# Two short groups of matmuls on a constant tile in the opening of a two-layer transformer kernel, and a new order of all its operations

## The chip, the cores and the metric

The kernel runs on one core of one Trainium2 chip. The core has a matrix engine (TensorE, in the profile PE, its weight loads PEld), a vector engine (VectorE, DVE), a scalar engine (ScalarE, ACT), GpSimd (POOL), and a queue on SyncE (SP) that starts the DMAs. Each engine works through its own list of instructions in order and waits on semaphores for the others. The metric is the time of one execution on the device in microseconds, less being better.

## What is computed

Two kinds of blocks are applied in turn, twice: sliding-window attention with 32 heads of 16 dimensions and a window of 256, and a token-mixing MLP across the 2048 positions.

```python
S, D, F, H, W = 2048, 512, 1792, 32, 256
def A(x):                                   # attention
    q, k, v = split(x @ wqkv)               # 32 heads of 16
    s = q @ k.T * 16 ** -0.5, kept where 0 <= i - j < W
    return softmax(s) @ v @ wo
def B(x):                                   # MLP over positions
    h = layernorm(x)
    u = gelu(einsum("sd,sf->df", h, w1) + b1)
    return (einsum("df,fs->ds", u, w2) + b2).T
for _ in range(2):
    x = x + A(layernorm(x))
    x = x + B(layernorm(x))
```

All inputs are bf16; x is 2048 by 512.

## The kernel before

x stays in SBUF as 16 blocks of 128 positions (`x_sb`). The program first builds a list of 2476 operations (`Graph.op`, line 107): an operation is one or several instructions of one engine, with the tiles that it reads and writes. The order in which they are put on the engines is not found when the kernel is built: the string `ORDER` (lines 15 to 42) holds a permutation of the list, and for each operation the choice among its alternative engines (`alts`: for example a copy on DVE or ACT, a mask on POOL or DVE). `begin_order` (line 44) unpacks it, `replay` (line 175) puts the operations on their engines in this order and gives out the buffers, and `emit` (line 196) works out the semaphore waits. So every engine's list, the DMA queue's included, follows from that string.

The stages. Attention goes by chunks of 64-position blocks (`CHUNKS`, line 331). For a chunk, `ln_blocks` (line 478) normalises blocks of x: `bn_stats` and `bn_aggr` on DVE, the power -1/2 on POOL (line 484), the subtraction and product on DVE (line 491) into `xh_sb`. `qkv` (line 535) transposes them into `xhT`, for the first 512 positions on PE (`f_tr`, line 547, four transposes of 128x128 into one PSUM bank, copied out at line 556 or 558 by DVE or ACT), later by DMA (line 542). Then `proj` multiplies by column blocks `o` = 0 to 3 of the weights of K and Q (line 513 is the matmul helper for all of these), and `vproj` by those of V. In the first layer the first 512 positions are handled in two halves of 256 (`split`, line 643).

`attention` (line 664) issues score groups (line 690), exponentials on ACT (line 705), masks on POOL or DVE (line 726), probability times value (line 747), a transposition and division by the sum (lines 767 to 778). There are 152 score groups in all. V reaches its layout `vb` by a store of four DMAs (line 636, operation `vz`). `wo_block` multiplies by `wo` and adds to x. Parts of the MLP's first product (`u_part`, line 842) and its second product (`y_block`, line 901) serve as other work for PE between score groups. `u_last` (line 861) is the rest of the first product with the gelu.

The opening. SP's first DMAs are `load_x` (line 400) and `load_w` (line 404). Weights are loaded in column parts: K and Q each as columns 0 to 255 (`o` = 0, 1) and 256 to 511 (`o` = 2, 3), V whole. SP's order in the string of before is: x block 1, x block 0, x blocks 2 and 3, K columns 0 to 255, Q columns 0 to 255, x blocks 4 to 7, Q columns 256 to 511, K columns 256 to 511, V, the two biases, x blocks 8 to 11, and so on. PE begins with `f_warm` (line 390), 36 matmuls of 128x128 on a tile of ones, a part of `uT` that the MLP overwrites much later. After them come, in the order of before: transposes of block 1, transposes of block 0, K o=0, Q o=0, Q o=1, K o=1, the first score group, transposes of block 3, transposes of block 2, Q o=3, the second score group, Q o=2, K o=2, the third score group, K o=3.

Of the kernel before, what the change touches and what calls it, by code (L numbers as in the profile page):

```python
# [11 lines left out]
P = 128  # L12


ORDER = (
    'c-qBQJ&5a87Cw^iym#m24ro9DE$D$>P@zHr1r$&~4;*kn0Tl{p!G#}q!G!|~IH1A-2lN&PwBQ9TIN-tyE*x;-!V50EV3sLdcwrV?xbVUhQ@EI7Sf+5{!o?nq'
    '$20ciz5Hx8yJyB%_g-CH-SeIAd`ALMAW$=FmRTW@UM>_MC=^Pi;EO_mPE}Ps8;@00Q*G-bFh2xcf8YPD^Jy4{4r?wJVNeNZF(i;5j)u<AALc&kTb8BtuoYXD'
    'EV9&YSZ!4!>!g`bN{ewkFV?-!CZqniE{d#Ft%9xV!b#)(TCEaPYV5=_a)q2Md&JD;Y}-<ZEX(4%qNtz|nGh-nqM(nNFd2`>41lrbFj=oV>y08w5=@sO5l;Q9'
    'E5~t`4k7c4g`?**4MwApcs`k)PYEH@>2%p2_m%ug%J;zU^<}w}Bmj_HTwbUu%%gUDrPRKHF)ZpZ8V-j>IkgT#q9zGxwOWL+*Q6H5QAD5FVugcBIS8UCVtAx5'
    'oJ<&u19$iv7cna1#_*YKJ5^OyJ|z~OtkC_q)3F@aao}aY-|XcJja+V-4ePd#=6Nr5$8=54^GwtKgfnf&d1+c%n=zA#x^CzI129br?M|l+Elo!hRD}YZf_Qqu'  # L20
    'SP)3ERD?p|W-T+p<AlWmmz&J>+$%~ixu#_`=S`xiFBAY-2B_6)1cnJql2x_3URO7ptD9B5K6*wd)Vkd{-aVgQFQ<Q>cFUdVVsW`#OsA3K%;)o&*{hi55Q9-J'
    '&$FfBG&||^{?_aDDLp%bAP7veKNy<kcP63}C9PHz{n0aH$ElgsxDhjE)LBq-b-g0Gt{ca(`sEk$b^TQ&DrE65;-xkz7100?E&w~1%|a*V<m_xVrnDCQ9!bX-'
    'm1YXX*h}M)fU!Om&@okIOl(PvC5<{j12J|S3bq}Tigu~!`;_{gMNNZdeg7q;j;bwzsGwS!B?u~0Ziq%Y!^?{V8oI8Zce{fD0`^>Em^H0dLzbj46plFn<Ww=A'
    'FQK`4LOj>DNP1RH&t|jQXq06s1sG+39kbi*t^uyE!Cc~!i-kgzrhK_Xo{tGG>%nMzHqPfML1rY`Bx!fr#C02P^EJAFZ(cjutY58xXXjs)hPF-A3lBL3pX4lJ'
    'o4RQ@9~cBgQ$#}$1OcwgE@B2$AdHBjArra3DN3SFkg5WD1k-axgz>l%2E(u)1b&%$CBINMT;FsZMb~r1oPiq~IYiJfbj!AeLw#WAgbe9`w0dBuuGqvgRI6$j'
    'Lc4<2z`#YeO+!o3Fn0_>IzT9qQcL7U7do+6@7L?yx^*Vrn%pXe80Su@MFqwhm|>=H;=0V37#a(!ArlQI2rlNJAe`WqOfhG#%;{=H-5W~sx^x5=7q*a+gflh$'
    'eZw$Pt#TZr6a%Qw`y4VQmouyne9JOS0EC7qvVzDPj44PKNl{G8B<pp1eIlAyme0J)%S%H$)eL|an)+N(`aLv4B*F~_HO#v|s2W6@$RDsi$nbjkB_tw<aCUYk'
    '2%!wcfUen!F_|78BN06ngymAB$TM;-Nt5|()|t)vvzaWn&qvv;Tm`7MhvtWaKA@`N30<K-=(ly9A_Jd|R8$)In<f)_y+1(=bS0n$TwlMwx<cq7j=u@(C`omM'
    's+WpyhcVx0`At5b6!LM*{CvrmDw0$xmkNc#rysW*%d#2dEs#FcKqmsA;wpwx&^1K`SfV3>fB;P<6ID1nqf~>FlQsVIBw?qUO$1{_QR7&{n2;j^pNrDz@KvRP'
    'TuK<mIr4oZ1y_!9SyUwYJ76btI<*!T3yU5b?QZw{9Hy=d9K2`0HxPs}^t#>t;Lp8&uVtQFrU}$Q`lqt{ZNl~Yf`ICa&~-Y75XsujO{=A87$B%rB7GV}b(9zY'  # L30
    '!{`(WoNg6MMP0AzkT0PA69N(@pXYm16Wzfq^z*(fYqEw}a{7X?cLkw<Ig%y~Rv3X&ok}t$2N6%!f^;N~$NkaC$qf0x1Uyf>-6bt(Dr%$g90?}?KF5_9Bjq&r'
    '9VRfOm7H#+>+RW`V$C>FkB<j`i7}q|K(_<XYPW`Ah;7)b*Etl+sQ&d=xDeCKb@TZ=swXnG*RcqAC>3m#2FEZ|10}nJyGwXDa!fJMLOcUE@4D;t8rCTF_KdDp'
    '|1^yA<<&pVaphmfWICUu<!>~UB*XY_G#-s?$tqjlN}AScVXSKL*K!D9S_VJ=yjH4~LRu`AgEE#cl(BpvpVe)WwLK4sNQCSM`bXp=iwJ^1G+BAkm!89|;E<#0'
    '5m!-^W`k?os-6+90>f~bsiaDi{tQqkm1!RJ6VNdN6KJ;<Xrpm^*cw#FsDIU@*6DORRU@vZyI^4JQ7JM?MU+}7R=i5t^UGK(hjfISwCi<9P;1@T^KGmPwx6?$'
    '*`}Si72oo#we1*=ty>Z<K|oE*NRs|kQo3VFj-qBWDr2RP%}Py=YhYMbK*X6DDpU<N!bV@P(lwST5xh&(i+Q7GS|c{pKw4GeK!HfSMw)Ln+D&j%-rOMigkF)W'
    'tIbAOU&8!+J`XM&6!y_r8jXS!q*_hOK?T1v(t@EBna)rd<f<%4h$aS4NQ;jOl%l*~OW_w9_o&0&&v3hj+gnZ!duhI<*Czn)Jlx^9hb0`)bV%+FN`XV$Zku+n'
    '%>ZN|?LN&sO}kq=zHOhv-X((zp6<=U-J8*Pa_H5QU5DrIHq7vcHy#^*d!K)d4tMK5e>l${9Ua~EIN<K_y7Py7!t>njX^wjX)W6uc-L~877SOvn4xM=XCjR#3'
    'ffxM4i0An?kYc;%9Wwk|$-{APJ07>ksr#_L-FWzK8n-+D0aDygj{&!b@9tr^=Pk!^+<%y7KZ6b2k1gcj|6*(}X#Cwjf54*cklzn(I)3MF&FvFM_fPP5OiFd)'
    'PDWB$dFT6#-?q>0yM*KRNS1zT!}g1NyGbT<D<hdyr!twhb1?I;1+K~*&h7>o9{)0XkL(?vf4BgDKjPoOZ+@F@{L_OaPq}pBkzPEK;jMa+EjG7q-XVq8Cxq-~'
    'fqY-CA5M)9kj(yDwjO2Pn4mw1SmuWW<UnaM{7ypdNwS?t+e|9Z`@ub6^$)5i|0od;xd4x4`DbU#p|J1k!A{$`U5U8saSyKSuRIv-&+SBsdzd5tlMLqG#I842'  # L40
    'njg9Q>mP6%x*dvl<9p-|jZg3K-1a{$!)bv|s~^WdEIxed;iHG!)%)G|$*<zszX32A5e)'
)

def begin_order(n):
# [208 lines left out]
def mm_cost(n, cols):  # L253
    return n * (cols / 2.4 + 4.0)
# [50 lines left out]
def bass_interleave_layers__sliding_block__mixer_token_mlp__prompt_kernel(  # L305
# [11 lines left out]
    S, D = A_x.shape[1], A_x.shape[2]  # L317
    F = B_w1.shape[1]
# [16 lines left out]
    with es:  # L335
# [9 lines left out]
        vb = sb("vb", [P, 3, 8, 16, 17])  # L345
# [6 lines left out]
        uT = sb("uT", [P, NFT, 512])  # L352
        w1b = sb("w1b", [P, 4, NT // 2, 256])
        w2b = sb("w2b", [P, 2, 4096])
        ident = sb("ident", [P, P])
# [14 lines left out]
        op = g.op  # L370
# [16 lines left out]

        warm = Tile(banks)

        def f_warm(e):  # L390
            for _ in range(36):
                last = e.matmul(PS[:, warm.slot, 0:P], lhsT=uT[:, 0, 0:P], rhs=uT[:, 0, 0:P], start=True, stop=True)
            return last
        op("vector:wm", lambda e: e.memset(uT[:, 0, 0:P], 1.0), writes=["uT0"], cost=100)
        op("tensor", f_warm, reads=["uT0"], writes=[warm], cost=2000, prio=-1, cfg="f", cls="f")

        x_src = A_x.rearrange("b (t p) d -> p (b t) d", p=P)
# [100 lines left out]
        def bank(t, i=0):  # L498
            return PS[:, t.slots[i], :]
# [7 lines left out]
        def fprio():  # L507
            return 1e6 + len(g.ops)
# [10 lines left out]
        def mm_group(kind, dst, n, mk, reads, cols=512, step=2, prio=None, holds=(), after=()):  # L519

            prio = fprio() if prio is None else prio
            for k0 in range(0, n, step):
                k1 = min(n, k0 + step)

                def f(e, cols32, k0=k0, k1=k1):
                    last = None
                    for k in range(k0, k1):
                        last = matmul(e, cols32, *mk(k), start=(k == 0), stop=(k == n - 1))
                    return last
                rd = reads(k0, k1) if callable(reads) else reads  # L530
                op("tensor:" + kind, f, reads=rd, writes=[dst], cost=mm_cost(k1 - k0, cols), prio=prio, holds=holds, after=after, cfg="f",
                   cls="f", flex=True)


        def qkv(m, before, split, layer):
# [3 lines left out]
            def transpose(i, wide):  # L539
                t = 4 * m + i  # L540
                if wide is None:
                    op("sync:tr", lambda e: e.dma_start_transpose(xhT[:, tx.slot, :, i * P:(i + 1) * P], xh_sb[:, t, :]),
                       reads=[f"xh{t}"], writes=[(tx, i)], dma=True, cost=1700, issue=1600.0, prio=-1e5)
                    return
                ft = filler(True)

                def f_tr(e):
                    for c in range(4):
                        last = e.transpose(bank(ft).bitcast(dt.bfloat16)[:, c * P:(c + 1) * P],
                                           xh_sb[:, t, c * P:(c + 1) * P], ident[:])  # L550
                    return last
                op("tensor:ftr", f_tr, reads=[f"xh{t}", "ident"], writes=[ft], cost=4 * 60, prio=fprio(),
                   holds=[tx], cfg="f", cls="f")
                src = lambda: bank(ft).bitcast(dt.bfloat16)[:, 0:512].rearrange("p (c n) -> p c n", c=4)
                dst = lambda: xhT[:, tx.slot, :, i * P:(i + 1) * P]
                op("vector:evt", lambda e: e.tensor_copy(dst(), src()), reads=[ft], writes=[(tx, i)],
                   cost=dve_cost(512, 0.5, psum=True), prio=-2e5,
                   alts=[("scalar", lambda e: e.copy(dst(), src()), act_cost(512))])

            def proj(o, which, a, b, wide):  # L560

                n, key = b - a, (filler(m == 0), which)
                ft = key[0]
                at = lambda: bank(ft)[:, 0:n]
                staged = m > 0 or (not layer and (o, a) in STAGED)
                ts = Tile(p_stg) if which and staged else None
                mm_group("fk" if which else "fq", key, 4, lambda c: (
# [75 lines left out]
            for a, b in ((0, 256), (256, 512)) if split else ((0, 512),):  # L643
                first = m == 0 and a == 0
                late_stats[:] = [first_k[0]] if m == 0 and not layer and not first else []
                before([4 * m + i for i in range(a // P, b // P)], first)
                late_stats[:] = []
                for i in range(a // P, b // P):
                    transpose(i, first if m == 0 and not layer else None)
                for which in (1, 0):  # L650
                    proj(0, which, a, b, first)
                vs = list(range(a // P, b // P))
                vproj(vs[0])
                for o in range(1, 4):
                    for which in (1, 0):
                        proj(o, which, a, b, False)
                if vs[2:]:
                    vproj(vs[2])
# [330 lines left out]
```

## Time and profile before

| | us |
|---|---|
| median of the runs of before | 437.09 |
| the runs | 437.09, 436.16, 437.51 |
| the profiled execution, its own time | 436.27 |
| span of that execution, first to last instruction | 434.5 |
| PE busy in the span | 420.9 |
| DVE busy | 322.6 |
| ACT busy | 317.0 |
| POOL busy | 187.2 |

The page of the profile gives busy times over the span, the granted TensorE clock in 40 slices (all of them at full speed here), the chain of work that ended last and the costliest groups of instructions. The timeline lists instructions in order of time, neighbours of one line merged, with the idle time of the engine before them and what ended it. The windows give each engine's busy time in a stretch. A matmul's record includes the time that its results need to drain, so PE shows as busy across small gaps; the starts of successive matmuls show the pace.

### The profile page before, as it was taken

To read this page: it belongs to the slowest core of one execution; us is meant where nothing else is said; L and a number is where in the kernel's file an instruction comes from. 1 tells how busy PE (TensorE), PEld (TensorE's weight loads), DVE (VectorE), ACT (ScalarE), POOL (GpSimd) and SP (SyncE) were. 2 spreads that over 40 slices of the span, in tenths; PEclk is the share of its full clock that TensorE was granted. 3 is DMA by queue.
4 is the path that set the end of the run, shared out by engine and by line. 5 is a ranking of instruction groups with operands and counts; after the bars stand their busy time and mean duration, and the time that the engine had idled before them with its cause. 6 is when DMAs were issued, how large, how long until landed. Compare 5 with 4: busy or idle time off the path is not lost.

```text
span 434.5 us, 14318 instructions
## 1 busy us (share of the span) xinstructions
PE 420.9 (97%) x6177; PEld 188.5 (43%) x6177; DVE 322.6 (74%) x629; ACT 317.0 (73%) x364; POOL 187.2 (43%) x277
## 2 busy tenths in 40 slices
PE   7979989999999999999999999999999999999997
PEld 6534333434444444444444444444434444445443
DVE  7998989779996678556777999989788758422205
ACT  5999999999997953606999999899999870520000
POOL 7788865864664620011465554365435221000000
PEclk9999999999999999999999999999999999999999
DMA  8565262302163257723542282240223262747713
GB/s 237 167 125 88 63 127 37 79 5 49 26 166 83 75 152 211 208 62 88 137 110 52 64 147 64 51 77 11 47 64 99 66 175 69 226 140 213 228 32 115
DMA packets 101850, 46.03 MB, mean 106 GB/s; under 512 B 32156, under 2 KB 101788, under 8 KB 101788
## 3 DMA queue, kind: packets, MB, share of 16 engines
q1 hardware_dynamic: 101788, 45.13, 41.7%
q8 instruction: 49, 0.80, 0.8%
q14 instruction: 13, 0.11, 0.1%
HBM read 33.56 MB, written 2.10 MB: 82 GB/s over the span
## 4 chain that ended last, share of the span: by engine, by line
PE 73%; ACT 18%; DVE 6%; DMA 1%; POOL 1%; issue 0%; SPq 0%
PE PS L513 50%; ACT pt L705 17%; PE PS L868 8%; PE PS L690 8%; PE PS L747 7%; DVE stats L471 1%; DMA vb<-vst 1%; DVE xh_sb L491 1%; DVE pt L726 1%; DVE rl L767 1%; DMA x_sb<-in_A_x_dram 1%; POOL pt L726 0%; DVE stg L594 0%; DVE vst L631 0%; SPq L636 0%
## 5 line engine op out<-in xcount | busy, mean ns | idle before, releaser
L705 ACT ACTIVATE pt<-PS 128x1024 bf16<-128x1024 f32 (+1 forms) x304 | 281.0, 1036 | 13.1 <-PE PS L690 11.9
L726 POOL TENSOR_TENSOR pt<-pt,ldm 128x256 int32<-128x256 int32 (+2 forms) x189 | 125.9, 686 | 101.7 <-ACT pt L705 101.1
L513 PE MATMUL PS<-xhT,wqkv 128*128 128x512 bf16 (+1 forms) x288 | 67.8, 357 | 2.7 <-ACT pt L705 1.9
L513 PE MATMUL PS<-xh_sb,w1b 128*128 128x512 bf16 x280 | 69.9, 381 | 0.1
L513 PE MATMUL PS<-uT,w2b 128*128 128x512 bf16 (+2 forms) x308 | 68.3, 360 | 0.0
L690 PE MATMUL PS<-qT,kbd 32*128 32x64 bf16 (+4 forms) x1552 | 60.2, 247 | 3.1 <-ACT pt L705 2.1
L484 POOL TENSOR_TENSOR rstd<-agg,mhalf 128x2 f32<-128x2 f32 (+1 forms) x33 | 23.8, 722 | 66.8 <-DVE agg L473 66.7
L909 DVE SCALAR_TENSOR_TENSOR x_sb<-PS,bcol,x_sb 128x512 bf16<-128x512 f32 x31 | 22.6, 746 | 38.0 <-PE PS L513 37.7
L690 PEld LDWEIGHTS PS<-qT,kbd 32*128 32x128 bf16 x1552 | 22.7, 92 | 61.7 <-ACT pt L705 45.6
L767 DVE STREAM_TRANSPOSE rl<-PS 128x1024 f32<-128x1024 f32 x32 | 39.9, 1248 | 12.3 <-PE PS L747 12.1
L747 PE MATMUL PS<-pt,vb 64*17 64x128 bf16 (+4 forms) x3104 | 43.6, 248 | 2.4 <-DMA vb<-vst 1.1
L471 DVE BATCH_NORM_STATS2 stats<-x_sb 128x6 f32<-128x512 bf16 x64 | 44.2, 693 | 1.5 <-DMA x_sb<-in_A_x_dram 0.8
L883 ACT ACTIVATE uT<-rl,bcol 128x512 bf16<-128x512 f32 x28 | 18.3, 712 | 33.8 <-DVE rl L879 33.8
L513 PEld LDWEIGHTS PS<-uT,w2b 128*128 128x128 bf16 x308 | 27.5, 98 | 31.1 <-issue 3.2
L747 PEld LDWEIGHTS PS<-pt,vb 64*17 64x17 bf16 x3104 | 31.8, 84 | 17.6 <-issue 7.9
L513 PE MATMUL PS<-uT,pt 128*128 128x512 bf16 x168 | 39.2, 379 | 0.0
L868 PE MATMUL PS<-xh_sb,w1b 128*128 128x512 bf16 x168 | 37.7, 379 | 0.0
L513 PEld LDWEIGHTS PS<-xhT,wqkv 128*128 128x128 bf16 x288 | 24.2, 97 | 30.1 <-issue 6.3
L513 PEld LDWEIGHTS PS<-xh_sb,w1b 128*128 128x128 bf16 x280 | 23.7, 98 | 30.8 <-issue 5.9
L513 PE MATMUL PS<-wqkv,xhT 128*128 128x512 bf16 x128 | 34.2, 381 | 0.2 <-DVE stg L594 0.2
L726 DVE TENSOR_TENSOR pt<-pt,ldn 128x256 int32<-128x256 int32 (+1 forms) x77 | 29.6, 404 | 5.3 <-ACT pt L705 5.0
L513 PE MATMUL PS<-wo_sb,oT 128*128 128x512 bf16 x128 | 32.4, 380 | 0.5 <-ACT pt L705 0.5
(62 smaller groups left out, 340.7 us busy)
## 6 DMA issues: line engine op xcount, KB each, us to landing
w1b<-in_B_w_dram SPq DMA_DIRECT2D x112, 128.0 KB, 2.8
w2b<-in_B_w_dram SPq DMA_DIRECT2D x70, 128.0 KB, 2.8
pt<-in_B_w_dram SPq DMA_DIRECT2D x42, 128.0 KB, 3.0
vb<-vst SPq DMA_DIRECT2D x64, 68.0 KB, 2.1
out_dram<-x_sb SPq DMA_DIRECT2D x15, 128.0 KB, 1.8
x_sb<-in_A_x_dram SPq DMA_DIRECT2D x3, 512.0 KB, 6.2
kbd<-stg SPq DMA_DIRECT2D x80, 16.0 KB, 1.9
wqkv<-in_A_wqkv_dram SPq DMA_DIRECT2D x4, 256.0 KB, 5.4
```

The lines of the kernel that those rows point to most:

```text
L471: op("vector:stat", lambda e: e.bn_stats(st[:, 0:6], x_sb[:, t, :]), reads=[f"x{t}"], writes=[("st", i)], cost=dve_cost(512))
L484: op("gpsimd:rstd", lambda e: e.tensor_tensor(rstd[:, t0:t1, 0], agg[:, t0:t1, 1], mhalf[:, 0:1].to_broadcast([P, t1 - t0]), op=ALU.pow), ...
L491: op("vector:xh", lambda e: e.tensor_scalar(xh_sb[:, t, :], x_sb[:, t, :], agg[:, t, 0:1], rstd[:, t, :], op0=ALU.subtract, op1=ALU.mult), ...
L513: return e.matmul(o, lhsT=w, rhs=x, start=start, stop=stop, skip_group_check=True)
L690: last = e.matmul(bank(tt[r // 2], r % 2)[:, base + c0 * 64:base + (c0 + n) * 64], lhsT=kbd[32 * r:32 * r + 32, tk.slot, o, jj].rearrange( ...
L705: op("scalar:exp", lambda e, ts=ts, tp=tp, i=i, cols=cols: e.activation(probs(tp)[:, i, 0:cols, :], pair(ts)[:, :, 0:cols].rearrange("p r ...
L726: return e.tensor_tensor(v, v, m, op=by)
L747: last = e.matmul(bank(t, h)[32 * r:32 * r + 17, i + q0 * 64:i + (q0 + n) * 64], lhsT=vb[64 * h:64 * h + 64, tk.slot, jj, 4 * o + r, :], r ...
L767: op("vector:od", lambda e, t=tod, tr=tr: e.transpose(rl[:, tr.slot:tr.slot + 2].rearrange("p a b -> p (a b)"), pair(t)), reads=[(tod, i) ...
L868: last = e.matmul(bank(tu, tt), lhsT=v()[:, sc - b0, k0 + tt * P:k0 + (tt + 1) * P], rhs=xh_sb[:, sc, :], start=(sc == b0), stop=(sc == NT ...
L883: op("scalar:gelu", lambda e, ft=ft, tt=tt: e.activation(uT[:, ft, :], rl[:, tmps[tt].slot], ACTF.Gelu_apprx_tanh, bias=b1col[:, ft:ft + 1 ...
L909: op("vector:resy", lambda e: e.scalar_tensor_tensor(x_sb[:, t, :], bank(ft), b2col[:, t:t + 1], x_sb[:, t, :], op0=ALU.add, op1=ALU.add), ...
```

## The change

Three things change in the code, and the order string.

- `f_warm` takes a count and a bank, and `warm_more` issues it as an operation of its own: two matmuls of 128x128 before the second of the first two transposes, into the bank that this transpose then overwrites, and six before the first projection (K o=0), into that projection's bank. The two are tied by `after` to the transpose before them, and by their bank to the work behind them.
- The first two blocks are transposed in the order block 1, block 0 in the program's list (`[::-1]`).
- The order string is another one. It holds two operations more.

```diff
-        def f_warm(e):
-            for _ in range(36):
-                last = e.matmul(PS[:, warm.slot, 0:P], lhsT=uT[:, 0, 0:P], rhs=uT[:, 0, 0:P], start=True, stop=True)
+        def f_warm(e, n=36, t=warm):
+            for _ in range(n):
+                last = e.matmul(PS[:, t.slot, 0:P], lhsT=uT[:, 0, 0:P], rhs=uT[:, 0, 0:P], start=True, stop=True)
             return last
         op("vector:wm", lambda e: e.memset(uT[:, 0, 0:P], 1.0), writes=["uT0"], cost=100)
+        first_tr = []
+
+        def warm_more(n, t, key):
+            op("tensor:wm2", lambda e: f_warm(e, n, t), reads=["uT0"], writes=[key], cost=56 * n, prio=fprio(), after=first_tr[-1:],
+               cfg="f", cls="f")
+
         op("tensor", f_warm, reads=["uT0"], writes=[warm], cost=2000, prio=-1, cfg="f", cls="f")
...
-                op("tensor:ftr", f_tr, reads=[f"xh{t}", "ident"], writes=[ft], cost=4 * 60, prio=fprio(),
-                   holds=[tx], cfg="f", cls="f")
+                begin = not layer and t < 2
+                if begin and first_tr:
+                    warm_more(2, ft, ft)
+                tr = op("tensor:ftr", f_tr, reads=[f"xh{t}", "ident"], writes=[ft], cost=4 * 60, prio=fprio(),
+                        holds=[tx], cfg="f", cls="f")
+                first_tr[len(first_tr):] = [tr] * begin
...
                 at = lambda: bank(ft)[:, 0:n]
+                if wide and which and not layer and not m:
+                    warm_more(6, ft, key)
...
-                for i in range(a // P, b // P):
+                for i in range(a // P, b // P)[::-1 if first and not layer else 1]:
                     transpose(i, first if m == 0 and not layer else None)
```

What the new string does, unpacked by the rule of `begin_order` and set against the old one:

- All 152 score groups keep their order. PE's list has as many changes between score groups, value groups and other matmuls as before (337). From the 9th score group on, the number of other matmul operations ahead of a score group is the same as before or differs by one to three.
- SP's first loads are now: x block 1, x block 0, x blocks 2 and 3, Q columns 0 to 255, K columns 0 to 255, K columns 256 to 511, x blocks 4 to 7, Q columns 256 to 511, V, one part of w1, x blocks 8 to 11, the biases. Ahead of the second store of V (`vz`) stand two parts of 128 KB (one of w1, one of w2) where `wo` (512 KB) and a part of w1 stood.
- PE's list opens with: transposes of block 1, the two matmuls, transposes of block 0, the six matmuls, K o=0, Q o=0, Q o=1, K o=1, the first score group, K o=3, transposes of block 3, Q o=2, transposes of block 2, Q o=3, K o=2, the second score group, Q o=2 of the second half, the third score group.
- The copy of block 0's transposes goes from ACT to DVE, that of block 2's from DVE to ACT. Over the whole kernel, masks on POOL go from 189 to 187 and on DVE from 77 to 79, but their places change: between the 81st and the 105th score group POOL has 16 masks instead of 31 and DVE 25 instead of 14.

More of the change, by code (lines that the diff above doesn't have):

```diff
@@ L15 @@
 ORDER = (
[L16 to L39, printed above, removed]
@@ L40 @@
-    'fqY-CA5M)9kj(yDwjO2Pn4mw1SmuWW<UnaM{7ypdNwS?t+e|9Z`@ub6^$)5i|0od;xd4x4`DbU#p|J1k!A{$`U5U8saSyKSuRIv-&+SBsdzd5tlMLqG#I842'
-    'njg9Q>mP6%x*dvl<9p-|jZg3K-1a{$!)bv|s~^WdEIxed;iHG!)%)G|$*<zszX32A5e)'
+    'c-pmAPl)5@6@Rk7+4&}X16t662DG4n3OXpD6de@s7A<It0t)EhfDR6*pn|se;1(SmFu?%_yx@Qe4!Gcg3of|efD118;DZA`xZuMa=HSB|rZ5K|T$sWf=3q*n'
+    '?HP}~vspGx^5&1Er|-{u@ArGZPmnN10ZP9&O<gBZE{-7xq9Du#;cs%efD#ycgW*6zQ)EK5dPDo5rhSn8)DcLl@q9L$`Gta&b#t=kWioa)o9SjcFRIUA+-$VI'
+    'Y&FfAM3&->EVkMrG>f9BNCo-nbT$o#)G#QeeJhMY(#>TWjcT<@=}{KV^@t>#2$@XAkR?eqgeQU|3$kQRFpkT~gb_*zfzvTwd0>6k>U5YO3iWb%KA(@S=5s+1'
@@ new lines @@
+    '*ka+ju6^<N+|Sb4IsTC0a7f1EF$|yx0He{U-=B7_eV<=gQnxDsI6@<tFXm7wDhkMFXK@K2pC<z=iUxxy>iw<Ljub^9P2Ap0@Ly69#cI{6#9x-nrBX>OU=pGz'
+    'Ggh2V*#wA}kD`c>APgKQ48zeVpUp?a{)9ZAPMen7j-L0Uux>jJsgP&BkM;93({`<_pEYyl3-iT`Ud}<|dCRtVQ6*%o5Jtk3VRX9P4zzW{G@kH0uW9u<!=!Ww'
+    'zfi%e2*;8n@W1wbe<4YpcLe+?BNI)dmSs^YgMNBieJW2X6+ysRKmbb#1y~je)$8kObx|l3=8ID4d=>;VXcZS%_4+AXPA)J1IhmYI>UICLHaT-=fn!XKkzq}v'
+    'Fr0_oCxdVM!)~uXwnn1Z7P`GI7TG{+H2!25*>*ddZ8n?b@*m5FQ9-k9yZEbWt@=4*u~sT;O!d5%ZXSy$%fgiq_@B|@`MK}M1wVcX;CaURiXI4*<8)lN)#4F;'
@@ new lines @@
+    'Cu4lXm<~)-6*`#+gdg&c2ZI66>$)uWXTJo-YV4%Oe^tdTu}Bo+qPejE3*>t~AqLSj;(dgyQYBf&i69Yx#R&SMD4w6sm$PnLR^-!Wx7*av##HE+2~-*l?x0Yt'
+    '33;IaaWe|@JOP?@vRLPy*Y@%rxJVdzG{V)8lt7PqnQj-EgX9J<uC5G&T`)GCo+1jAes?xI1NaBt(IKUcey<DldaM5DZ|e2BlYB$$q@D;?)v}AESSpqX@#U$Z'
+    '$eOM)&FfN?wrraUl1hv1a{Ejnph)ujK#-C$;>>P%rj;%MRK^JD)Y?V`!XP6%E9MkS<v3=bMBs(lTmVklAhHC8ESE!GGuo2kx^j`1EXz?;Sr$cAReS1W(jAXO'
+    'Nz|K?h%sW0ktkG3rM9IcQr3(j&kV{XL`<+O$fzW*cxVchhl-|6i8vm2sy<%<QfG`I?$uhY#-xhWZs!_}EaMsb+Vk=Si#am;oaYMy?r%M2$HB@ljrRq9PTA!G'
@@ new lines @@
+    '2{9NreUI;YkB4pN6W6nnB;kW<^?AZF8FtK=ss<VJSjm2feDvVM52+<s8Ozdj9T0r!fLDL<SePoZ@DyOVTx$9gb+K6JbL<Z1eMv%UAlpF3W^1->TR<XLj(CAD'
+    '7L^(YvQqLZ%gT*hJji^0aB^|-I}!DS4}wsE9P@=wg$RxUCbFBG8$sZlg{snv739*{cs3g%Pfv;TbUdw`nkIJfU_5C+2e^J1Qlv8d3w4|cv;Nw`ZW=41q(i^|'
+    '>eVay^{WH8fos63#c{QIc6K?9E2v2#V?7b!?DXrsM*U^-TSf75OwI*Grn)X_lEv(gUv&JOzfzYD<FU5@G*!*0C^Q!Gb1BhPSx(@|F`I~!$wZtYi&ug6udm_g'
+    'ga@_WOq!RM+P@l@ldi7hkdTrn!XG3VCe3CLJZ3%u$oMvjsBI_VOCCO>ENnCpS9LH@k?gA4YEd@9^uPw_cE9ZnuqZi7IpruxzG*Z8@u`3PswN|x*g#z@f3M5b'
@@ new lines @@
+    'TDelWX<nhJDlFpoyjD$;S~VV3;<yZ87E2}}l!n-Hfu!2D>kv*xzhQt*byOuwt57PnWSQ!^pz8&yX?pPA&u~0pc*@}U!Ru635MWV6$jFr_4Ee!eu{gkl*bKFx'
+    '(`hJ5LLd?G0OiXi0om~dN3z)4uFLb3DXT*S<2~Xi#Y1B{#S|vVa4y&W-s|;y0G$q$Tjc?8&}hc>xE&|0R?Bs<U$QvVvLZZ&S;o%ff!bsxS32SCjB1*ync)>Y'
+    'S4bf*3QUqE!jlz*2qJ+i@*nfx$fBijL-o^0znm|^;JeWXhN74mPRa{K6k8yu&1S2G3atv5Myp+^txkfk;#T>qFB@^O#=webSS*GiK&084rOJU7<UR$}{P>yo'
+    '+>G6fZ9hW|02LAX02pf4)03efJf^^15podMrFu;ym_L^jbfkJ$Q5;XC>n>8&Sid<tRU7RhqCgZ$g39QkJX;?{h1iEM?A3dnLOWln6v}2&2!ebmzxpyExKj>!'
@@ new lines @@
+    '3w{nJfd_gPvc7FwD5oSLx_%8A%l26|Dr7Yk39V*(Og9zPk{m&EBn{<VazIge@upjqBvGLKWno!uFBSlbuXxvsD=~K?DA#-_U0qpf$u$?oIi(jDi;MZia+$DY'
+    'bu_xX8I(=aBg^GAac9vyDwo~y)GZd-WEkLQhl`&>2!;+xt-m%GP!6!bxJyI;<umryZ~<h&W2ldWV63XPZX!|4imN=?s;CsT8dhHTQO0o(JzL+S9rwZBW%F^c'
+    'e@9o*zF`Ay<s|Dhx%GbNI$YncZV%I|{Wv&;!*qHz=J4=vHU4;Kjg@2ba>qyR19$`}oRPZU{LzE(A3m-vb$da(yML`Z+}ldFF4f)d-QbOHZzlI9l(_E)W&Msz'
+    'zXdgJy8^cjiQ8cJhIKK!b$Y4Po^zdZ3M;o4RO&v8{i=Kq*B<V<TZy-4`i_?RQ7dr&_q2Pcw_UN$mfHd0Co*mq&!5+hf52GwR%dGSw`v~-TaK;m{^hpAQoGbk'
@@ L42 @@
+    'y#{b<Q`HT1?n}SvFm6X|?u)eck@w!a6G1|5=NxU`rZ<|gx}^8?YJHndZ??D{b6fVip4;!e^$O{G?{4^;O;Y!{?)FS-+kOxFFqJxd(DJt_6K*eA%!};x*e3DY'
+    'tRHRe-`Je#y?ZPKxs5lSzSGk*q~C^rIt_0gu-Pw_g8dBliLs|Ou;mAA`LPwPI~jfVhTUl0dd0o@dzHMGAnu1M1@}gEyWNVr4S>6o`yJWaKHQOaSFE`$%XhV!'
+    '+djRkvZQ~K<DPq$l6-$KKbur>uQ$bQakxETc51x&xvln^6!?(3Lx<aC!glT*Hr#`JxQD9z)7k$3;XEYV'
 )
@@ L530, in mm_group @@
                 rd = reads(k0, k1) if callable(reads) else reads
-                op("tensor:" + kind, f, reads=rd, writes=[dst], cost=mm_cost(k1 - k0, cols), prio=prio, holds=holds, after=after, cfg="f",
-                   cls="f", flex=True)
+                op("tensor:" + kind, f, reads=rd, writes=[dst], cost=mm_cost(k1 - k0, cols), prio=prio, holds=holds,
+                   after=after, cfg="f", cls="f", flex=True)
         def qkv(m, before, split, layer):
```

## The prediction

> **What bounds the kernel now.** The page first: which engine is full, and which engines the chain that ended last runs through.
>
> ```profile
> PE 420.9 (97%) x6177; PEld 188.5 (43%) x6177; DVE 322.6 (74%) x629; ACT 317.0 (73%) x364; POOL 187.2 (43%) x277
> ...
> PE 73%; ACT 18%; DVE 6%; DMA 1%; POOL 1%; issue 0%; SPq 0%
> ```
>
> PE bounds the whole, but 18% of the chain is ACT. The windows say where (span, then busy time of PE, PEld, DVE, ACT, POOL):
>
> ```profile
> 10.00:20.00 10.00, 9.55 (x117) 5.64 (x114) 9.94 (x28) 9.97 (x16) 8.55 (x16) 1.00 0.67 192
> ...
> 60.00:80.00 20.00, 18.24 (x424) 7.71 (x420) 16.88 (x32) 20.00 (x23) 12.73 (x19) 1.00 0.42 84
> ...
> 160.00:180.00 20.00, 20.00 (x94) 8.96 (x93) 16.36 (x29) 7.94 (x13) 0.69 (x1) 1.00 0.75 206
> ```
>
> ```profile
> 209.70:226.20 16.50, 16.50 (x269) 6.91 (x268) 11.87 (x22) 15.83 (x20) 8.63 (x14) 1.00 0.51 120
> 226.20:242.00 15.80, 15.80 (x265) 6.57 (x264) 12.79 (x24) 15.22 (x19) 10.40 (x16) 1.00 0.25 62
> 242.00:258.00 16.00, 16.00 (x315) 6.97 (x314) 15.59 (x35) 15.43 (x17) 7.35 (x11) 1.00 0.45 105
> 258.00:274.00 16.00, 16.00 (x237) 6.55 (x228) 15.66 (x33) 14.96 (x18) 9.69 (x15) 1.00 0.35 55
> ```
>
> From about 9 to 118 us ACT is full and PE has the holes; what ACT loses there, the end loses. From 118 us PE is full. In the second layer's attention DVE is nearly full too (15.66 of 16.00).
>
> Then the opening, where the change lies, first PE's timeline (the 36 matmuls, transposes of block 1, of block 0, projections, scores, transposes), then one row of PEld's:
>
> ```profile
> 1.10 4.02 PE L392 MATMUL PS<-uT 128*128 128x128 bf16 x36 [1.10 <-DVE stats L465]
> 5.08 0.40 PE L549 MATMUL PS<-ident,xh_sb 128*128 128x128 bf16 x4
> 5.95 0.40 PE L549 MATMUL PS<-ident,xh_sb 128*128 128x128 bf16 x4 [0.47 <-DVE xh_sb L491]
> 7.11 1.91 PE L513 MATMUL PS<-xhT,wqkv 128*128 128x256 bf16 x16 [0.77 <-ACT xhT L558]
> 8.95 0.40 PE L690 MATMUL PS<-qT,kbd 32*128 32x256 bf16 x12
> 9.71 0.62 PE L549 MATMUL PS<-ident,xh_sb 128*128 128x128 bf16 x8 [0.37 <-DVE xh_sb L491]
> ```
>
> ```profile
> 10.37 0.33 PEld L513 LDWEIGHTS PS<-xhT,wqkv 128*128 128x128 bf16 x4 [0.21 <-DMA wqkv<-in_A_wqkv_dram]
> ```
>
> PE waits twice (0.47 and 0.77 us) where the new groups go, and at 10.37 for a load: that is Q's columns 256 to 511. Last, ACT's timeline up to its first idle time after 9.40, and PE's wait ahead of that:
>
> ```profile
> 6.38 0.59 ACT L558 COPY xhT<-PS 128x512 bf16<-128x512 bf16 x1 [0.28 <-PE PS L549]
> ...
> 9.40 2.51 ACT L705 ACTIVATE pt<-PS 128x1024 bf16<-128x1024 f32 x3
> ...
> 34.57 1.94 ACT L705 ACTIVATE pt<-PS 128x1024 bf16<-128x1024 f32 x2 [0.68 <-PE PS L690]
> ```
>
> ```profile
> 32.65 1.52 PE L747 MATMUL PS<-pt,vb 64*17 64x64 bf16 x128 [1.06 <-DMA vb<-vst]
> ```
>
> **The change, part by part.** The sum is made on the profiled execution: 436.27, its span 434.5 and 1.77 around it. The median of the runs shown is 0.82 above.
>
> *The two groups.* A 128-column matmul takes (4.02 - 0.29) / 35 = 0.107 us in the first 36, where 0.29 is the record of a single one, and (0.62 - 0.23) / 7 = 0.056 in the transposes at 9.71, by the same reckoning. Two cost 0.11 and six 0.34 us at the second pace, 0.21 and 0.64 at the first. They fill holes of 0.47 and 0.77 us, wait only for the ones written at 0.88 us and for banks nobody has used, and what stands behind them on PE (block 0's transposes, K o=0) waits longer for DVE and ACT: 0 us. If the holes were gone they would cost 0.45 us. The clock is at full pace from 5.08, so in this execution they gain nothing either.
>
> *The copies of the first transposes.* Block 0's copy is now DVE's, behind one more `bn_stats`: 5.89, the end of block 0's normalisation, + 0.59 (the statistics' pace in the chain of waits) + 0.40 (a DVE copy, from the two in 0.73) = 6.88, where ACT ended at 6.97. But K's first columns are now fifth among the loads, and the fifth landed at 7.06 by the trace's landing records. So K o=0 still starts near 7.1: 0 us, between -0.1 and +0.1.
>
> *The loads and PE's list behind the first scores.* This is the term that I take to decide. The landing records of before, in order of issue, end at 2.98, 3.39, 4.78, 5.57, 7.06, then x blocks 4 to 7 at 9.42, Q's second columns at 10.33, K's second at 11.14, V at 12.52: in the order in which SP issued them, all issued by 5.42. In the new order Q's second columns are eighth, behind the bytes of the first seven, which together with their own make the same 2,048 KB that had landed at 11.14. Now Q o=2 stands right behind block 3's transposes on PE, with block 2's transposes, Q o=3, K o=2 and the second scores queued behind it. PE: Q o=2 at 11.17 to 11.61 (four of 0.109, as 16 take 1.91), transposes to 11.84, two projections to 12.72, a change of form 0.15, second scores at 12.87; before it was 10.97. ACT ends its first two exponentials at 11.30, then has block 2's copy, which can begin 0.43 after its transposes (5.95 to 6.38): 12.04. It ends at 12.63, Q o=2's copy at 13.00, and the second exponentials begin 0.45 after their scores (as 8.95 to 9.40), 13.32. ACT is idle 0.74 + 0.32 = 1.06 us where it was full, and has 0.59 us of copy that DVE had.
>
> DVE loses as well: its list has the statistics of blocks 6 and 7 ahead of the copy of block 3, and x blocks 4 to 7 now land at about 10.33 (1,792 KB) instead of 9.42, against 9.55 when DVE gets there. What is late by that hangs behind the same ACT work.
>
> Something comes back at 34.57. That wait of 0.68 us is for the store `vz`, issued behind 640 KB of `wo` and w1; now 256 KB stand there. At the 385 GB/s that the DMA view shows between 28 and 31 us this is 1.0 us less, and ACT comes later anyway, so the 0.68 goes. Net: 1.06 + 0.59 - 0.68 = 0.97 us. Low end: were Q's columns to land at 10.33 after all, ACT would idle 0.25: 0.16. High end: nothing comes back, 1.65. I take 0.97, since the landings of before are in issue order throughout.
>
> *The rest of the order.* PE's list is nearly the old one, so what can differ is who is late for it. I added up the work that stands ahead of each score group on DVE, each operation at the median of its kind in the trace. Between the 81st group (209.7 us) and the groups at 254 to 270 us the new order puts 7.4 us more on DVE (8.5 at the worst group), mostly masks that POOL had, and takes it back by 290. DVE's idle time from 209.7 to 262 is 4.63 + 3.01 + 0.41 + 0.1 = 8.1 us. Its fullest window leaves 2% idle; at that, 7.0 of the 8.1 can be used, and 7.4 - 7.0 = 0.4 us is over. Worst group: 1.5 us. Other way: by the starts of its matmuls against their pace, PE loses 4.0 us between 200 and 345; if half of that went, -2.0. I take 0.4, because DVE is so full in the very rows into which the work comes.
>
> Sum: 436.27 + 0 + 0 + 0.97 + 0.4 = 437.64. The runs' median lies 0.82 above the profiled execution for a reason that its trace can't show; I carry half of it, 0.41, with ends of 0 and 0.82: **438.05 us, or 438.0**.
>
> A rule that bears on that half. In this trace the pace changes from 0.107 to 0.056 between the matmuls at 4.81 and 5.08. The Trainium skill, page "TensorE: Matmul & The Clock Gate", Part 1, says that the clock is released after a busy window of about 3.4 us and that this window runs freely, whatever the kernel does. The one release at 5.0 us agrees with it; no single trace can show the rest.
>
> **The rivals.**
>
> 1. *The clock.* In some executions of before, the pace may stay at 0.107 through the first projections, because PE is idle for 0.47 and 0.77 us just then, and the new groups end that. The spread of 1.35 us between the runs speaks for it: 16 projection matmuls of 0.109 us at half the pace are 16 x 0.1 = 1.6 us more. Against it: in the one trace the pace never drops. Then the offset of 0.82 goes, and if the new order is worth nothing, 436.3 is left. By the page's rule just named the release would in such executions come at the next window's end.
> 2. *DVE becomes the bound of the second layer* (slower). Place: 210 to 270 us. It decides once the added work exceeds the 7.0 us that DVE has to spare; the worst group has 8.5. Price 1.5: 436.27 + 0.97 + 1.5 + 0.41 = 439.15. For it: 15.59 and 15.66 of 16.00. Against: masks on DVE are shorter (438 ns against 743 on POOL), so single results come earlier.
> 3. *The new order removes PE's small waits* (faster). DVE has 6 us less between 262 and 290 us, where the chain of waits runs through DVE from 258 to 276. Opening at its low end, half of the 4.0 us gone: 436.27 + 0.16 - 2.0 + 0.41 = 434.8. Against: PE is busy 16.00 of 16.00 there.
>
> That the groups do nothing, the clock being full already, is inside the forecast: with the whole offset it is 438.5.
>
> **How the numbers follow.** Forecast 0.45, with its own range from 436.9 to 439.0; clock 0.10; DVE 0.25; faster 0.20. The range: low 436.27 - 0.1 + 0.16 - 1.2 = 435.1 (part of the third rival), high 436.27 + 0.1 + 1.65 + 1.5 + 0.82 = 440.3. 0.3%, about what a measurement of this kernel can tell from no change, is 1.3 us: faster is below 435.78, slower above 438.40. The forecast lies close to that line, so 0.17 of its 0.45 is slower. Slower: 0.17 + 0.25 = 0.42. Faster: 0.20 and 0.02 of the clock's case, 0.22. Within: 0.36.
>
> **What would show it.** In the changed profile: the group of two and that of six inside PE's waits before 7.1 us, K o=0 still near 7.1; a wait of PE of over 1 us for `wqkv` that ends near 11.1; the second score group near 12.9; ACT idle about 1 us between 11 and 13.5; no ACT wait near 34 us; DVE at 98% or more from 210 to 260 us with PE waiting there. The forecast is wrong if the second scores come by 11.5, if ACT's late opening is made up before 118 us, or if PE's waits in 200 to 345 us change by more than 2 us either way.

## The result, and the profile after

The changed kernel takes 440.43 us (median; runs of 439.24, 440.65, 440.43, 441.18 and 439.30) against 437.09 (437.09, 436.16, 437.51, 437.45 and 436.42). The ratio is 1.0078, 95% interval 1.0057 to 1.0099: slower by 3.3 us, 0.13 us above the upper end of the predicted range. The profiled execution of after is the 439.24, 2.97 above that of before; its span is 437.5.

The page of after, the same two lines (some of PE's records are missing in this trace, 6119 of 6185 are there, so that its busy time is some us too low, and holes where a record is missing count as `issue`):

```profile
PE 413.0 (94%) x6119; PEld 187.9 (43%) x6185; DVE 326.3 (75%) x640; ACT 316.7 (72%) x364; POOL 181.3 (41%) x268
...
PE 70%; ACT 19%; DMA 4%; SPq 3%; issue 2%; DVE 0%
```

In the chain of waits DMA has gone from 1% to 4% and SP's queue from nothing to 3%; DVE has gone from 6% to nothing. So the chain now runs in part through transfers and through the queue that issues them; what that costs, the waits below say.

The opening of after, PE's timeline, then PEld's row for Q's second columns, then ACT's timeline:

```profile
5.04 0.40 PE L555 MATMUL PS<-ident,xh_sb 128*128 128x128 bf16 x4
5.27 0.28 PE L392 MATMUL PS<-uT 128*128 128x128 bf16 x2
5.91 0.40 PE L555 MATMUL PS<-ident,xh_sb 128*128 128x128 bf16 x4 [0.36 <-DVE xh_sb L497]
6.14 0.50 PE L392 MATMUL PS<-uT 128*128 128x128 bf16 x6
7.17 1.91 PE L519 MATMUL PS<-xhT,wqkv 128*128 128x256 bf16 x16 [0.53 <-DMA wqkv<-in_A_wqkv_dram]
9.01 0.40 PE L702 MATMUL PS<-qT,kbd 32*128 32x256 bf16 x12
```

```profile
10.28 0.33 PEld L519 LDWEIGHTS PS<-xhT,wqkv 128*128 128x128 bf16 x4 [0.28 <-DMA wqkv<-in_A_wqkv_dram]
```

```profile
9.46 1.94 ACT L717 ACTIVATE pt<-PS 128x1024 bf16<-128x1024 f32 x2
11.29 0.59 ACT L568 COPY xhT<-PS 128x512 bf16<-128x512 bf16 x1
11.76 0.40 ACT L586 CAST qT<-PS 128x256 bf16<-128x256 f32 x1
12.27 1.09 ACT L717 ACTIVATE pt<-PS 128x512 bf16<-128x512 f32 x2
...
19.42 23.97 ACT L717 ACTIVATE pt<-PS 128x1024 bf16<-128x1024 f32 x26
```

The groups (L392 at 5.27 and 6.14) lie inside PE's waits, and the first projection starts at 7.17 (7.11 before). Q's second columns hold PE until 10.28, not 11.1. ACT goes from one instruction to the next with hardly a hole (0.11 us between 9.4 and 13.5), and from 19.42 to 43.4 without one: the wait of 0.68 at 34.57 has gone. Compared operation by operation, by the semaphore that each one raises, the first score group ends 0.06 us later than in before, the second 0.96 later (12.25), the ninth 0.10 later, at 34 us after is 0.63 ahead, and at 151 us still 0.37. The opening costs nothing.

What costs is this, PE's timeline of after in two stretches of the MLP's products (L880 and L519 with `w1b`, `w2b`):

```profile
129.42 1.90 PE L519 MATMUL PS<-xh_sb,w1b 128*128 128x512 bf16 x8 [0.52 <-DMA w1b<-in_B_w_dram]
...
170.25 2.97 PE L880 MATMUL PS<-xh_sb,w1b 128*128 128x512 bf16 x13 [0.69 <-DMA w1b<-in_B_w_dram]
173.73 1.02 PE L880 MATMUL PS<-xh_sb,w1b 128*128 128x512 bf16 x4 [0.51 <-DMA w1b<-in_B_w_dram]
```

```profile
218.25 0.60 PE L519 MATMUL PS<-uT,w2b 128*128 128x512 bf16 x2
220.09 1.04 PE L519 MATMUL PS<-uT,w2b 128*128 128x512 bf16 x4 [1.24 <-DMA w2b<-in_B_w_dram]
```

Four weight loads come late. By the landing records and the pace of the matmuls ahead, PE could have gone on 0.68, 0.63, 0.58 and 1.40 us earlier, 3.3 us together, had it waited for nothing else; for the first of the four that isn't so, as the experiments show. The lag behind before goes from -0.4 to +1.7 over the first three and to +3.1 behind the fourth, and stays between 2.5 and 3.4 from 284 us to the end. In before the same stretch has no wait at all (29 matmuls in a row from 165.87, in its PE timeline):

```profile
165.87 6.44 PE L868 MATMUL PS<-xh_sb,w1b 128*128 128x512 bf16 x29
```

SP issues one DMA at a time, some 0.5 us each in these traces. The fourth load stands at place 147 of SP's list where it had place 118; it was issued at 215.99 and landed at 220.05, where before issued it at 177.12.

The windows of after that answer to those shown of before (span, then busy time of PE, PEld, DVE, ACT, POOL):

```profile
160.00:180.00 20.00, 18.80 (x88) 8.18 (x87) 16.81 (x29) 8.12 (x13) 0.69 (x1) 1.00 0.63 179
```

```profile
209.70:226.20 16.50, 14.78 (x260) 6.22 (x261) 14.14 (x29) 14.14 (x18) 4.39 (x7) 1.00 0.58 141
226.20:242.00 15.80, 15.48 (x196) 6.36 (x197) 14.29 (x30) 15.31 (x19) 4.04 (x7) 1.00 0.21 53
```

PE has lost 1.2 us in the first and 1.7 in the second; the late loads at 170, 173 and 219 us lie there. DVE has more work from 209.7 us, as reckoned (14.14 against 11.87), and still leaves 2.4 us idle.

### The profile page after: what moved, and what is told of

Its sections match the earlier page's. It is cut to its first block, busy times and chain, and to the rows that moved or that the text cites. A ratio compares the mean times of both kernels' runs of the same rounds, so it can differ in the third digit from the quotient of the medians.

```text
span 437.5 us, 14271 instructions
## 1 busy us (share of the span) xinstructions
PE 413.0 (94%) x6119; PEld 187.9 (43%) x6185; DVE 326.3 (75%) x640; ACT 316.7 (72%) x364; POOL 181.3 (41%) x268
## 4 chain that ended last, share of the span: by engine, by line
PE 70%; ACT 19%; DMA 4%; SPq 3%; issue 2%; DVE 0%
PE PS L519 50%; ACT pt L717 19%; PE PS L880 8%; PE PS L702 7%; PE PS L759 6%; DMA w1b<-in_B_w_dram 2%; DMA wqkv<-in_A_wqkv_dram 1%; SPq L827 1%; DMA w2b<-in_B_w_dram 1%; SPq L815 1%; SPq L648 1%; SPq L407 0%; SPq L411 0%; SPq L548 0%; ACT kbd L594 0%
## 5 line engine op out<-in xcount | busy, mean ns | idle before, releaser
L519 PE MATMUL PS<-xhT,wqkv 128*128 128x512 bf16 (+1 forms) x274 | 64.8, 355 | 5.6 <-ACT pt L717 3.4
L519 PE MATMUL PS<-xh_sb,w1b 128*128 128x512 bf16 x263 | 66.1, 380 | 3.3 <-issue 2.1
L519 PE MATMUL PS<-uT,w2b 128*128 128x512 bf16 (+2 forms) x299 | 67.1, 360 | 2.2 <-DMA w2b<-in_B_w_dram 1.2
L477 DVE BATCH_NORM_STATS2 stats<-x_sb 128x6 f32<-128x512 bf16 x64 | 43.2, 680 | 1.5 <-DMA x_sb<-in_A_x_dram 0.8
L519 PEld LDWEIGHTS PS<-uT,w2b 128*128 128x128 bf16 x308 | 27.7, 98 | 33.4 <-issue 3.1
L519 PE MATMUL PS<-uT,pt 128*128 128x512 bf16 x163 | 39.3, 379 | 0.3
L880 PE MATMUL PS<-xh_sb,w1b 128*128 128x512 bf16 x165 | 37.6, 379 | 1.3 <-DMA w1b<-in_B_w_dram 1.2
L519 PEld LDWEIGHTS PS<-xh_sb,w1b 128*128 128x128 bf16 x280 | 23.4, 97 | 31.8 <-issue 6.3
L519 PEld LDWEIGHTS PS<-xhT,wqkv 128*128 128x128 bf16 x288 | 23.7, 97 | 30.8 <-issue 7.2
L519 PE MATMUL PS<-wqkv,xhT 128*128 128x512 bf16 x118 | 32.0, 380 | 1.4 <-issue 1.0
L519 PE MATMUL PS<-wo_sb,oT 128*128 128x512 bf16 x120 | 31.1, 380 | 1.7 <-DVE pt L738 0.7
```

The source lines that it names most:

```text
L477: op("vector:stat", lambda e: e.bn_stats(st[:, 0:6], x_sb[:, t, :]), reads=[f"x{t}"], writes=[("st", i)], cost=dve_cost(512))
L519: return e.matmul(o, lhsT=w, rhs=x, start=start, stop=stop, skip_group_check=True)
L880: last = e.matmul(bank(tu, tt), lhsT=v()[:, sc - b0, k0 + tt * P:k0 + (tt + 1) * P], rhs=xh_sb[:, sc, :], start=(sc == b0), stop=(sc == NT ...
```

## The experiments

The median of before differs a little from one batch of runs to the next (436.67, 436.89 and 437.08 us), so ratios are compared, each with the runs of before in its own batch.

**The late loads.** The order string is the new one, but some weight loads have other places in SP's list. Each of the three w1 loads has changed places with the load that stood where it now stands, and the w2 load moved up alone; no other operation moves.

```diff
-SP place 65:  w1 that PE waits for at 129 us
+SP place 61:  the same
-SP place 101: w1 that PE waits for at 170 us
+SP place 94:  the same
-SP place 108: w1 that PE waits for at 173 us
+SP place 102: the same
-SP place 147: w2 that PE waits for at 219 us
+SP place 114: the same
```

> The changed kernel with four DMA issues at other places of SP's queue, nothing else: the w1 load of the first operand at 128.7 us goes four places forward, two w1 loads of u_last seven and six places, one w2 load from 216 us to behind the load at 175 us. Late loads (theory): the changed kernel's trace shows PE waiting 0.68 + 0.63 + 0.58 + 1.40 = 3.3 us for just these four, each beyond the time at which PE had ended the work before; all of it goes: profiled execution 439.24 - 3.3 = 435.9, median 437.1 if its distance of 1.2 to the profiled execution stays. DVE as the bound of the second layer (rival): 438 to 439 still, PE waits elsewhere in 200 to 270 us. Nothing: 439.2 to 440.4.

> The changed kernel with only the one w2 load moved from 216 us to behind the load at 175 us. Late loads: 1.4 us less, profiled 437.8, and the score groups behind 221 us 1.4 us earlier than in the changed kernel. DVE bound: the wait at 218.9 us goes, and comes back on another operation before 270 us: 439.2.

> The changed kernel with only the three w1 loads moved. Late loads: 0.68 + 0.63 + 0.58 = 1.9 us less, profiled 437.4; if the waits before 200 us are made up again by the wait at 218.9 us (a load that lands at a fixed time), only part of it, 438.0 to 439.2: that load is issued behind copies that PE releases, so I expect the whole 1.9.

Measured: all four moved 438.59 us, ratio to before 1.0036 [1.0014, 1.0059]; the last alone 439.60, 1.0052 [1.0031, 1.0073]; the three others alone 439.88, 1.0068 [1.0044, 1.0092]. The profiled executions took 436.39, 439.78 and 437.85, each more than expected (435.9, 437.8 and 437.4). PE's timeline with all four moved, at 129 us and at the place of the waits at 170 and 173 us:

```profile
129.25 1.89 PE L519 MATMUL PS<-xh_sb,w1b 128*128 128x512 bf16 x8 [0.36 <-issue]
...
167.65 6.64 PE L880 MATMUL PS<-xh_sb,w1b 128*128 128x512 bf16 x30
```

The waits for these loads have gone, and in this execution all but 0.12 us of the loss. At 129 us PE still stands, for nothing that the profile shows, and goes on only 0.17 us earlier than in after (129.25 against 129.42). So of the 0.68 us there at most some 0.2 were the load's; the four loads make about 2.8 us, and 439.24 - 436.39 = 2.85. The medians, by their ratios, say something else: 1.8 us of the loss are won back, 1.6 stay, and the runs spread from 436.39 to 440.99. So the loads are a cause, shown, and there is another one, of which this execution has little. With the last load alone the wait at 219 goes, but that execution lost 0.5 us in the opening and 0.6 more by 45 us, and a load of w2 was 0.66 us late at 255 us: once PE gets there earlier, the next load is the late one.

**The groups.** The new order without the groups, the old order with them, and the new order with the four loads moved and without the groups.

```diff
-                    warm_more(2, ft, ft)
...
-                    warm_more(6, ft, key)
```

> The kernel before with its own order, and the two groups of 2 and 6 matmuls put in at the places that the change gives them. Groups hidden in PE's waits: profiled 436.3, median as before within 0.5. Clock (rival): the runs of before that lie at 437.1 to 437.5 come down to 436.2: median 0.8 lower and the spread under 0.5. Groups on the path: 0.1 to 0.5 us more.

> The changed kernel's order without the two groups of matmuls. Putting the groups into the old order took the median up by 1.8 us, in its trace 0.4 us by 34 us and 2.1 us by waits for loads at 129, 161 and 400 us. Groups on the path (theory): 1 to 1.8 us below the changed kernel, 438.6 to 439.4. Groups hidden, and the waits for loads a matter of how the loads fall in each execution: as the changed kernel, 440.0 to 440.6.

> The new order with the four loads moved, without the two groups. With the groups its median was 438.6 and its profiled execution 436.4. Groups on the path: 436.8 to 437.6, level with the kernel before. Groups hidden: 438.6 as with them. If it comes below 436.3, this is the version that beats both.

Measured: the old order with groups 438.43 us, 1.0037 [1.0022, 1.0051]; the new order without 439.11, 1.0042 [1.0019, 1.0065]; the loads moved and no groups 436.60, 0.9997 [0.9979, 1.0015]. The groups cost about 1.6 us in either order (1.0037 against 1; 1.0078 against 1.0042; 1.0036 against 0.9997; in the last two pairs the intervals overlap a little, but the three agree), and the moved loads bring the rest back. In the old order that is more than any of the three cases expected. Eight matmuls that lie in waits of PE and delay little there cost 1.6 us.

**Each group alone, in the old order.**

> The kernel before with only the group of two matmuls. If the groups cost by their place, the six in front of the first projection do it, and two between the transposes cost nothing: 436.7. If any added instruction shifts it (two would do as well as eight): 438.4.

> The kernel before with only the group of six matmuls ahead of the first projection. If the place costs: 438.4, as with both. If neither group costs and the 1.8 us with both were the loads' doing: between 436.7 and 438.4 without any rule.

Measured: the two alone 437.17 us, 0.9994 [0.9978, 1.0009]; the six alone 437.75, 1.0014 [0.9995, 1.0033]. The intervals overlap, but the traces helped. With the six, PE's timeline has a wait that the trace of before doesn't show:

```profile
127.65 0.41 PE L700 MATMUL PS<-qT,kbd 32*128 32x64 bf16 x24
127.99 0.82 PE L519 MATMUL PS<-xh_sb,w1b 128*128 128x512 bf16 x3
129.70 1.67 PE L519 MATMUL PS<-xh_sb,w1b 128*128 128x512 bf16 x7 [0.89 <-issue]
```

Three of ten matmuls of one product run, then PE stands for 0.89 us and waits for nothing that the profile shows, 120 us behind the group. The old order with both groups has such waits too, after the first of the same ten and at 162 us; an expectation above took them for waits for loads. That led to another theory: not the place of the groups counts but their number, as every TensorE instruction ahead shifts the later ones in the stream that is fetched.

The profiled execution of the two alone shows something else: its clock came late. PE's timeline:

```profile
6.01 0.61 PE L555 MATMUL PS<-ident,xh_sb 128*128 128x128 bf16 x4
7.38 3.40 PE L519 MATMUL PS<-xhT,wqkv 128*128 128x256 bf16 x16 [0.77 <-ACT xhT L568]
10.72 0.40 PE L700 MATMUL PS<-qT,kbd 32*128 32x256 bf16 x12
```

The 16 projections take 3.40 us instead of 1.91. The clock's record begins at 10.48 us (at 5.01 in before); the first scores end 1.77 us late, and 1.50 is left at the end.

**Number or place.** Three kernels settle it. In the first the groups stay where they are in the old order, but the first warm-up does the same columns in eight matmuls fewer. In the second there are no groups, and the first warm-up does the same columns in eight matmuls more. The third is the new order with the loads moved, both groups in, and the shorter warm-up. The loop of 28 is that of the first and third kernel, where the tile of ones is also filled over 256 columns instead of 128 for the wider matmuls to read; the loop of 44 is that of the second.

```diff
-            for _ in range(36):
-                last = e.matmul(PS[:, warm.slot, 0:P], ...)
+            for k in range(28):
+                n = 2 * P if k < 8 else P
+                last = e.matmul(PS[:, warm.slot, 0:n], ...)
...
+            for k in range(44):
+                n = P // 2 if k < 16 else P
+                last = e.matmul(PS[:, warm.slot, 0:n], ...)
```

> The order of before with both groups at their places (as e4_before_groups), but the first warm-up has 28 matmuls in place of 36, eight of them 256 columns wide instead of 128: as many columns as before, and with the two groups exactly as many TensorE instructions as before. Theory 'stream': the groups cost time because 16 more TensorE instructions (8 matmuls, 8 weight loads) ahead of everything shift where the instruction stream is fetched, so that the engine waits for nothing the profile shows in the middle of a run (0.89 us at 129 us in e8_before_group_of_six). Then this kernel goes like before: ratio 1.000 (within 0.0015), and no such wait over 0.3 us that before has not. Theory 'place': the groups themselves, between the first transposes and the first projection, delay something. Then it goes like e4_before_groups: ratio 1.0037 (1.0022 to 1.0051), 1.6 us over before.

> Before without any group, but the first warm-up has 44 matmuls in place of 36, sixteen of them 64 columns wide instead of 128: as many columns as before, 16 more TensorE instructions (8 matmuls, 8 weight loads) ahead of everything, as the groups bring. Theory 'stream': like e4_before_groups, ratio 1.0037 (1.0022 to 1.0051), with TensorE waits for nothing the profile shows near 129 or 162 us. Theory 'place': like before, ratio 1.000 (within 0.0015). If both g1_groups_same_count and this one are near 1.000, the groups cost by place and count together, or by how loads happen to land; if both are near 1.0037, each alone is enough.

> e1_four_loads (the new order with its four late weight loads moved up in SP's queue, both groups in) with the same 28 matmuls in the first warm-up, so that TensorE has as many instructions as before. Theory 'stream': like e6_four_loads_no_groups, ratio 0.9997 (0.998 to 1.0015). Theory 'place': like e1_four_loads, ratio 1.0036 (1.0014 to 1.0059).

Measured: groups with the number kept 436.29 us, 0.9984 [0.9970, 0.9998]; no groups and 16 instructions more 438.77, 1.0039 [1.0025, 1.0054]; the new order with the loads moved and the number kept 437.07, 0.9993 [0.9977, 1.0010]. All three go by "stream", none by "place"; the first lies 0.0001 outside the band given for "stream", on the lower side. It has the lowest ratio of all kernels measured here, 0.16% ahead of before, but its interval nearly reaches 1 and overlaps those of the next ones. PE's timeline of the second kernel, and of before at the same work:

```profile
128.32 0.41 PE L695 MATMUL PS<-qT,kbd 32*128 32x64 bf16 x24
128.66 0.39 PE L518 MATMUL PS<-xh_sb,w1b 128*128 128x512 bf16 x1
130.03 2.10 PE L518 MATMUL PS<-xh_sb,w1b 128*128 128x512 bf16 x9 [0.98 <-issue]
...
161.65 0.38 PE L518 MATMUL PS<-xh_sb,w1b 128*128 128x512 bf16 x1
162.89 0.39 PE L518 MATMUL PS<-xh_sb,w1b 128*128 128x512 bf16 x1 [0.86 <-issue]
```

```profile
128.06 0.41 PE L690 MATMUL PS<-qT,kbd 32*128 32x64 bf16 x24
128.40 2.33 PE L513 MATMUL PS<-xh_sb,w1b 128*128 128x512 bf16 x10
```

One run of ten became one, a hole, and nine. The page has a queue that fits, and every kernel's page has these 49 packets:

```profile
q8 instruction: 49, 0.80, 0.8%
```

They are of 16 KB each. PE has 12,565 records in the second kernel (6185 matmuls, 6185 weight loads, 195 others), which is 256 to a packet. Counted from the start, the matmul behind the first hole is the 2361st in all three kernels of the old order that have it. The first record behind the second hole, the weight load of the 2995th matmul in the two that have it, comes 1,280 PE records later, which is 5 x 256. This table is put together from the trace's start times and the DMA records of q8:

```
old order                more instr.  2361st  gap ahead  after the last q8 packet's end
before                        0       130.35    0.22        2.09
groups, number kept           0       130.37    0.22        2.25
group of two                  4       131.05    0.22        2.18
group of six                 12       129.70    1.27        1.38
both groups                  16       130.21    0.62        1.49
no groups, 44 matmuls        16       130.03    1.37        1.43
```

At this place PE goes on about 1.4 us after the end of a q8 packet and not before. With 16 instructions more it gets there eight matmuls of 0.22 us earlier in its work, 1.7 us, and has to wait; with four more it just need not.

The other traces agree. Twelve of the thirteen have all of PE's records, and in them the page finds no releaser for 13 waits of PE over 0.2 us, apart from one of 0.56 at 21 to 22 us that every one of these kernels with the new order has. All 13 lie a multiple of 256 records from the 4802nd, which in the old order is the 2361st matmul (counted in the program's order, to one record), and 12 of the 13 are in kernels with 12 or 16 instructions more. At no such edge of any of the twelve traces does PE go on earlier than 1.19 us after the packet's end. The wait at 129 us in after stands at such an edge too: PE goes on 1.37 us after a packet's end, just as the load has landed.

That the packet holds PE's next 256 instructions is my reading of these counts, the profile doesn't say it. The two holes make 1.15 + 1.02 = 2.17 us (gaps of 1.37 and 1.24 less the pace of 0.22) of the 3.3 us by which this execution lags at the end; of the rest 0.3 had come by 126 us, 0.3 come between 165 and 370 us and some 0.5 after 375, and I haven't followed them to a cause.

## Why the prediction was wrong

Slower was the likelier side in it, with 0.42, and slower it is; but the loss is 3.3 us where the sum's terms make 1.4, and none of these terms is its cause. That the side came out right is luck: what made the forecast lean to it, the opening and DVE, cost nothing that the trace shows.

- **The two groups, 0 us.** Right at their place: both inside PE's waits, the first projection 0.06 us later. Wrong as a price. The step counted what the matmuls take and what stands right behind them, and not that 16 instructions more shift PE's whole stream. Measured: 1.6 us in either order, nothing if the number of instructions is kept. The range took this term at 0 (the 0.45 stands beside it and is in neither end). No wait of PE in before is put down to `issue`, but q8 was on the page.
- **The copies of the first transposes, 0.** Right, and for the reason given: 7.17 against 7.11, behind the load of K's first columns.
- **The loads behind the first scores, 0.97.** Wrong. The step assumed that Q's second columns, with the same bytes ahead of them as the eighth load of before, land at the same 11.14. They landed at 10.24, V at 11.75 instead of 12.52, and x blocks 4 to 7 at 9.43, not 10.33. ACT idled 0.1 us, not 1.06, as it had copies to do in the meantime, and the 0.68 at 34 us came back as predicted. The term came out below its low end of 0.16: by 34 us after was 0.63 ahead. By its own test ("if ACT's late opening is made up before 118 us") the forecast was wrong at 34 us already.
- **The rest of the order, 0.4.** The step that failed most. It looked for the late partner only on DVE. DVE did get the work, and had room: from 221 to 270 us the lag of single score groups scatters between 2.1 and 4.1 us, with no trend. But the order string orders SP's queue too, and I had followed that only through the opening. Four loads became late, where PE in before waits for no load of w1 or w2: about 2.8 us in the trace (3.3 with the wait that falls together with an edge of the stream), about 1.9 in the medians (1.0078 to 1.0036 with groups, 1.0042 to 0.9997 without).
- **Half of the offset, 0.41,** and the first rival. The rival's clock exists: one trace, that of the group of two in the old order, caught it late, at a price of 1.77 us in the opening (1.6 reckoned). That it makes the offset of before, and that the groups end it, is not shown. The Trainium skill, "TensorE: Matmul & The Clock Gate", Part 1, has it that the window runs freely: the releases seen here at 4.15 to 6.49 us and once at 10.48 agree. With the number of instructions kept the groups alone bring 0.16% (interval 0.02 to 0.30%), to 436.29 us; the rival had 436.3. That the two agree is partly luck: the rival took the added instructions to cost nothing, and that holds only with their number kept. None of those 12 runs is above 437.01 us; of the 28 of before beside them 14 are. That they gain by the clock fits, but I have no trace of a late clock in before.
- **The second and third rival.** DVE didn't become the bound. The small waits of PE in the second layer didn't go.

So by the medians the 3.3 us are about 1.9 for late loads and 1.6 for the shifted stream, and the new order is worth nothing that can be told (0.9997 and 0.9993 with both mended).

## What to carry to other kernels

Where an order is found anew, go through each queue to its end, the DMA queue first: for each prefetch its issue, its landing and the earliest time that its first user could start, since the loads with least to spare decide. A few instructions added at the start of a long unrolled program can cost far from their place; try the same work with the same number of instructions before you judge what they do. And one trace doesn't stand for the median: with the loads moved, the trace lost 0.12 us and the median 1.6.

## What the runs showed of the hardware

- PE can stand where no semaphore holds it, as read here for its own instructions. There is one packet of 16 KB on q8 for 256 of PE's records, and where PE reaches the edge less than some 1.2 to 1.5 us after the packet's end, it waits: up to 1.15 us at one edge, in the midst of products at full pace.
- The clock's release differs between executions: 4.15 to 6.49 us in eleven traces, 10.48 in one (a thirteenth has no record of it). The records of full clock last 426.67, 430.08 or 433.49 us, in steps of 3.41. The granted clock that each run lists is 0.995 or 0.996 in 21 of 90 runs of before, and in 3 of 77 of the seven kernels run beside it that hold the group of six. In the last 28 runs of before, those at 0.996 have a median of 437.6 us, the others 436.5. Half pace through one window of about 3.4 us, as that page of the Trainium skill has it, would be 0.4% of 430 us, which is what 0.996 shows; but the one trace with a late release lists 1.000, its record beginning with the release, so that the two needn't be the same case.
- The same 2,048 KB took until 11.14 us in one order and until 10.24 in the other, and the first 1,792 KB until 10.33 and 9.43. The bytes ahead alone don't give the landing time of a load in the opening; why the two orders differ stays open.
